# A recurrence with two dense layers: four more weight tiles converted behind the recurrence, and a new order on the vector engine and in the chunk loads

## The chip, the cores and the metric

One core of one Trainium2 chip runs the whole program. The metric is the device time of one execution in microseconds. Three executions of the kernel before took 1266.93, 1270.55 and 1269.22 us, with a median of 1269.22 us.

## The reference

Inputs are six tensors r, k, v, w, a, b of shape (4, 8, 768, 40) and the weights of two dense layers. Everything is float32 in the reference.

```python
# recurrence, for each batch and head; state is 40 x 40, t runs over 768 steps
y[t]  = r[t] @ state
Sa    = state @ a[t]
state = state * w[t][None, :] - outer(Sa, b[t]) + outer(v[t], k[t])
# x: y with heads side by side, 3072 tokens x 320
h = x @ w_in;  g = max(h, 0) ** 2;   x = g @ w_out     # first layer, 320 -> 2048 -> 320
h = x @ w_in2; g = h * cos(h);       out = g @ w_out2  # second layer, same sizes
```

The weights can arrive as float64, and then a 64-bit word is turned into a float32 on the chip by integer operations; this is the case here.

## The kernel before

**Recurrence.** The 768 steps are cut into 12 chunks of 64. Within a chunk the steps are put into matrix form, and a small triangular system per head has to be solved. `Program.period(c)` writes out chunk c as 42 slots; a list `todo` says which function is called in which slot. As no scheduler changes this order, an engine works through its instructions just as the calls emit them, and an instruction that waits holds up all that stand behind it on its engine or DMA queue. Nearly all DMAs are issued by SyncE (SP), so they form one list too.

In slots 0 to 16 and 20 to 36 the state update of chunk c runs in two halves (`Attn.state`, five stages each: tiles `pq`, `px`, `pu`, `py`, `pm` on TensorE, with ScalarE and VectorE between). In the same slots other chunks are prepared. For chunk c+1: the last Gram matrices (`gt`, tile `pgt`) are computed in slot 0 and masked by VectorE in slots 1 and 2, then written to DRAM (`gt_out`, tile `Ls`, slot 3) and read back in another layout (`solve_load`, tile `L`, slot 6). The triangular solve (`solve`, lines 472 and 475, 62 small operations and a copy) runs from slot 9 to slot 36, on VectorE for c = 0 and on GpSimd (POOL) after that. Its result goes to DRAM and back (`solve_store` and `load_t`, tiles `Tn`, `Ts`, `t`, `tt`, slots 37 and 38), and `merge` (tiles `pw`, `pt`) uses it in slot 2 of the next period. For chunk c+2: `load_kb` (line 362, 832 KB into `cin`, slot 7), `compact_kb` on VectorE (slots 10 to 16, line 404), `load_a` (slot 13). For chunk c+3: `load_w` (slot 30) and the first part of its decay products.

**Dense layers.** `Mlp.pipeline` handles 512 tokens at a time: six blocks for the first layer and then six for the second. Each block has 16 steps f, one for each 128 hidden units: 8 matmuls into `h` (input and weight are split into a high part and a rest, `xh`, `xl`), the activation (ScalarE and, for the rest `gl`, POOL), and two steps later the output matmuls `out(q - 2)`. The generator yields after pairs of matmuls; a period takes 64.2 of these yields, spread over its slots. The first layer's block b becomes ready after chunk 2b+1. `split_x` splits a block's input when the block before is at its last step: three ScalarE copies to `xh` and three VectorE subtractions to `xl`, in turn. Functions in `self.later` are called after a number of yields.

**Weights.** A tile is one f of one layer, 128 x 704 values. The first layer's tiles are converted in the first periods (`first`, `rest`). From the second layer's 16 tiles, `second` converts tiles 0 to 7 during the recurrence, in four pieces each: load (tile `w`), two ScalarE operations (lines 169 and 170), three VectorE operations (line 144 is the helper through which VectorE's instructions are recorded), one POOL addition (line 181), a store to DRAM (`w2f`, line 281). One piece starts every 5 steps of this generator, which is stepped in every slot for c = 2 and 3 and in every second slot after that. `load_w2` reads these tiles back in the first layer's last block. Tiles 8 to 15 are converted by `late` behind the recurrence, whole, one every 14 yields (tile `wr`), while the first layer's last block runs. `split_w2` splits each tile two steps ahead of its use in the second layer's first block: three VectorE and three POOL operations.

## Time and profile before

| What | us |
|---|---|
| median of three executions | 1269.22 |
| the profiled execution | 1271.16 |
| its span, first to last instruction | 1269.3 |
| start and periods 0 and 1, without dense layers | 0 to 211 |
| periods 2 to 10, with the first layer's blocks | 211 to 792 |
| period 11 | 792 to 843 |
| first layer's last block | 843 to 918 |
| second layer | 918 to 1262 |

TensorE is busy for 84% of the span, VectorE and ScalarE for 55% each and POOL for 52%. The granted TensorE clock is 0.905 on average: 0.61 to 0.95 in the periods, and full from period 11's end on. A period ends here where the store of the solve's result (`Tn`, line 485) is issued: at 69.9, 133.7, 211.4, 281.1, 348.1, 415.3, 479.0, 546.3, 607.7, 670.5, 732.4 and 792.3 us.

### The profile page before, as it was taken

What the parts mean: (1) busy time and instruction counts of PE and PEld (TensorE: products, weight loads), DVE (VectorE), ACT (ScalarE), POOL (GpSimd) and SP (SyncE); (2) the same over time, 40 slices, a digit from 0 to 9 for tenths busy, and PEclk for the clock granted to TensorE, in tenths of its full rate; (3) what the DMA queues carried; (4) which work ended last, traced back from release to release, by engine and by line L of the source; (5) the groups of instructions that cost most, each with busy time, mean ns of one, the idle gap of its engine ahead of it and who ended that gap; (6) DMA issues with size and microseconds to landing.
All of it is one profiled execution on the core that took longest, in us unless ns stands there. A gap on an engine that the chain in (4) does not pass through costs nothing.

```text
span 1269.3 us, 26741 instructions
## 1 busy us (share of the span) xinstructions
PE 1071.2 (84%) x10242; PEld 900.0 (71%) x10242; DVE 702.9 (55%) x1378; ACT 696.4 (55%) x1444; POOL 663.2 (52%) x1043
## 2 busy tenths in 40 slices
PE   3245626788979898988988989999999999999997
PEld 3144525666757676867776767777889999999996
DVE  6869856666655565655564543124696343443432
ACT  4133633656655556654846466447756565655553
POOL 4112486595938382848484838126796333333332
PEclk9985655788988888988989889899999999999999
DMA  6473653637282727463747262236201010100000
GB/s 177 89 166 100 152 140 65 139 87 149 60 187 83 150 66 156 104 132 87 159 105 148 54 137 71 58 99 216 70 12 46 1 47 1 47 13 34 1 22 25
DMA packets 271952, 115.96 MB, mean 91 GB/s; under 512 B 229990, under 2 KB 250982, under 8 KB 270670
## 3 DMA queue, kind: packets, MB, share of 16 engines
q1 hardware_dynamic: 269979, 113.47, 37.6%
q8 instruction: 83, 1.36, 0.4%
q10 hardware_dynamic: 1834, 0.69, 0.2%
q14 instruction: 56, 0.45, 0.1%
HBM read 88.42 MB, written 25.69 MB: 90 GB/s over the span
## 4 chain that ended last, share of the span: by engine, by line
PE 48%; POOL 20%; DMA 11%; DVE 10%; issue 5%; SPq 4%; ACT 2%; POOLq 0%; ACTq 0%; DVEq 0%
PE h L863 21%; PE pt L809 13%; POOL T L475 7%; PE po L819 6%; POOL ttmp L472 6%; DMA cin<-cin 6%; POOL gl L720 3%; POOL u L181 2%; DMA xf<-xs 1%; PE px L597 1%; DVE T L475 1%; DVE ttmp L472 1%; DMA t<-Tn 1%; DVE cin L144 1%; PE pu L605 1%
## 5 line engine op out<-in xcount | busy, mean ns | idle before, releaser
L863 PE MATMUL h<-xh,ws 128*128 128x512 f32 x960 | 332.1, 409 | 20.2 <-ACT g L717 18.0
L863 PE MATMUL h<-xl,ws 128*128 128x512 f32 x576 | 234.9, 408 | 0.5 <-DVE xl L144 0.5
L863 PEld LDWEIGHTS h<-xh,ws 128*128 128x128 f32 x960 | 184.9, 194 | 62.6 <-ACT g L717 20.1
L748 POOL TENSOR_TENSOR gl<-g,gh 128x512 fp32r<-128x512 f32 x96 | 125.1, 1303 | 191.0 <-ACT gh L747 158.9
L720 POOL TENSOR_TENSOR gl<-g,gh 128x512 fp32r<-128x512 f32 x96 | 126.8, 1320 | 186.5 <-ACT gh L719 146.0
L819 PE MATMUL po<-gh,ws 128*128 128x512 f32 x480 | 143.1, 422 | 1.9 <-ACT o L767 1.3
L472 POOL TENSOR_TENSOR ttmp<-T,L 128x126 f32<-128x126 f32 (+22 forms) x310 | 124.1, 400 | 35.7 <-DMA L<-Ls 15.3
L475 POOL TENSOR_TENSOR T<-T,ttmp 128x126 f32<-128x126 f32 (+22 forms) x310 | 128.7, 415 | 20.1
L717 ACT ACTIVATE g<-h 128x512 f32<-128x512 f32 x96 | 57.2, 596 | 134.2 <-PE h L863 92.5
L809 PE MATMUL pt<-ws,gh 128*128 128x320 f32 x768 | 128.1, 308 | 0.5 <-DVE g L144 0.4
L863 PEld LDWEIGHTS h<-xl,ws 128*128 128x128 f32 x576 | 111.9, 194 | 21.3 <-DVE xl L144 1.1
L181 POOL TENSOR_TENSOR u<-u,w 128x384 int32<-128x384 int32 (+2 forms) x72 | 54.7, 760 | 136.9 <-DVE u L144 108.9
L809 PEld LDWEIGHTS pt<-ws,gh 128*128 128x128 f32 x768 | 119.9, 188 | 8.3 <-DVE g L144 0.6
L144 DVE SCALAR_TENSOR_TENSOR g<-n,h 128x512 f32<-128x512 int32 x96 | 66.0, 688 | 103.2 <-ACT n L728 100.4
L728 ACT ACTIVATE n<-h 128x512 int32<-128x512 f32 x96 | 57.3, 596 | 119.9 <-PE h L863 119.8
L431 PE MATMUL pgt<-at,cin 40*128 40x104 f32 x768 | 70.7, 325 | 51.8 <-DVE at L144 21.0
L819 PEld LDWEIGHTS po<-gh,ws 128*128 128x128 f32 x480 | 94.0, 202 | 25.9 <-ACT o L767 1.9
L144 DVE TENSOR_SCALAR u<-u 128x160 f32<-128x160 f32 (+9 forms) x144 | 50.5, 351 | 99.7 <-ACT u L169 88.9
L144 DVE TENSOR_TENSOR g<-g,h 128x512 f32<-128x512 f32 x96 | 65.8, 685 | 71.7 <-ACT g L732 71.7
L144 DVE TENSOR_TENSOR mov<-pu,kc 64x416 f32<-64x416 f32 x96 | 56.5, 588 | 83.8 <-PE pu L606 81.4
L431 PEld LDWEIGHTS pgt<-at,cin 40*128 40x128 f32 x768 | 60.9, 226 | 58.6 <-issue 24.3
L819 PE MATMUL po<-gl,ws 128*128 128x512 f32 x288 | 85.9, 402 | 0.0
(104 smaller groups left out, 2310.2 us busy)
## 6 DMA issues: line engine op xcount, KB each, us to landing
w<-moe SPq DMA_DIRECT2D x20, 704.0 KB
rv<-rv SPq DMA_DIRECT2D x48, 256.0 KB
cin<-cin SPq DMA_DIRECT2D x11, 832.0 KB
Ls<-ga SPq DMA_DIRECT2D x48, 128.0 KB
L<-Ls SPq DMA_DIRECT2D x48, 128.0 KB
cin<-cin SPq DMA_DIRECT2D x11, 422.5 KB
at<-cin SPq DMA_DIRECT2D x11, 416.0 KB
mov<-vt SPq DMA_DIRECT2D x96, 40.0 KB
```

What stands on the lines that cost most here:

```text
L144: fn(*args, **kwargs)
L181: self.nc.gpsimd.tensor_tensor(t.bitcast(I32), u.bitcast(I32), w[:, :, 0], op=ALU.add)
L431: nc.tensor.matmul(pv[par][:, j], self.kb[r0:r0 + 40, p0 + j].rearrange("p h b -> p (h b)"), self.at[r0:r0 + 40, p0 + j], start=True, stop ...
L472: eng.tensor_tensor(tv, T[:, 0:r, j:j + 1].to_broadcast([128, r, n]), L[:, j:j + 1, j + 1:32].to_broadcast([128, r, n]), op=ALU.mult)
L475: eng.tensor_tensor(T[:, 0:r, j + 1:32], T[:, 0:r, j + 1:32], tv, op=ALU.add)
L717: nc.scalar.activation(g, h, AF.Relu)
L720: self.later.append((2, lambda: nc.gpsimd.tensor_tensor(gl, g, gh, op=ALU.subtract)))
L728: nc.scalar.activation(n, h, AF.Copy, bias=0.25, scale=float(np.float32(1.0 / (2.0 * np.pi))))
L748: nc.gpsimd.tensor_tensor(gl, g, gh, op=ALU.subtract)
L809: nc.tensor.matmul(self.pos[j][:, 0:DM], x[:, 128 * j:128 * j + 128], wo[:, DM * ws:DM * ws + DM], start=(f == 0 and x is gh and ws == 0), ...
L819: nc.tensor.matmul(self.pos[m], wo[:, 128 * ws:128 * ws + 128], x, start=(f == 0 and k in (0, 2, 4)), stop=(f == NF - 1 and k in (5, 6, 7)))
L863: nc.tensor.matmul(h, wi[:, ws], x[:, kt], start=(k == 0), stop=(k == 7))
```

## The change

`LATE` counts the tiles that `second` converts; it goes from 8 to 4, so `late` converts tiles 4 to 15. `load_w2` follows, as it reads back tiles below `LATE`. The vector operation that clamps a weight's high word moves from `clamp` to `bits`, for all weights, and the pieces' `bits` and `add` come one step later. `split_x` for the first layer (but for the very first block) puts its three subtractions off by four yields. The pipeline issues `out(q - 2)` ahead of the `h` matmuls at f = 0 of a first-layer block (not the first) instead of behind them; the list `later` no longer lets an entry that is not due hold up those behind it. `load_kb` moves from slot 7 to slot 1, `load_a` from 13 to 11, `load_w` from 30 to 18.

```diff
-LATE = 8
+LATE = 4
@@ class Weights: clamp, bits
         nc.scalar.activation(w[:, :, 0], w[:, :, 0].bitcast(U32), AF.Copy, scale=2.0 ** -29)
+
+    def bits(self, w, u):
+
+        hi, ui = w[:, :, 1], u.bitcast(I32)
         self.vec.tensor_scalar(u, u, LOW_WORD, HIGH_WORD, op0=ALU.max, op1=ALU.min)
-
-    def bits(self, w, u):
-
-        hi, ui = w[:, :, 1], u.bitcast(I32)
@@ pieces
-            return [(0, load), (4, clamp), (5, lambda: self.bits(st["w"], st["u"])),
-                    (6, lambda: self.add(st["w"], st["u"], st["u"])), (period + 5, lambda: end(f, c0, st["u"]))]
+            return [(0, load), (4, clamp), (6, lambda: self.bits(st["w"], st["u"])),
+                    (7, lambda: self.add(st["w"], st["u"], st["u"])), (period + 5, lambda: end(f, c0, st["u"]))]
@@ class Mlp: split_x(self, layer, blk, wait=0)
             nc.scalar.activation(xh[:, kt], xs[kt], AF.Copy)
-            self.vec.tensor_tensor(xl[:, kt], xs[kt], xh[:, kt], op=ALU.subtract)
+            if not wait:
+                self.vec.tensor_tensor(xl[:, kt], xs[kt], xh[:, kt], op=ALU.subtract)
+        if wait:
+            def low():
+                for kt in range(3):
+                    self.vec.tensor_tensor(xl[:, kt], xs[kt], xh[:, kt], op=ALU.subtract)
+
+            self.later.append((wait, low))
@@ stream
-                while self.later and self.later[0][0] <= 0:
-                    self.later.pop(0)[1]()
+                due = [fn for n, fn in self.later if n <= 0]
+                self.later = [z for z in self.later if z[0] > 0]
+                for fn in due:
+                    fn()
@@ pipeline
-            self.split_x(*steps[q][:2])
+            self.split_x(*steps[q][:2], 0 if steps[q][0] else 4)
...
             if q < len(steps):
+                if f == 0 and q and layer == 0:
+                    yield from out(q - 2)
...
-                if q >= 2:
+                if q >= 2 and (f or layer):
                     yield from out(q - 2)
@@ class Program: period
-            at(7, A.load_kb, c + 2)
-            at(13, A.load_a, c + 2)
+            at(1, A.load_kb, c + 2)
+            at(11, A.load_a, c + 2)
...
-            at(30, A.load_w, c + 3)
+            at(18, A.load_w, c + 3)
```

## Rows read from the trace of the kernel before

**Rows 1.** Page, part 4: shares of the chain that ended last, by engine.

```profile
PE 48%; POOL 20%; DMA 11%; DVE 10%; issue 5%; SPq 4%; ACT 2%; POOLq 0%; ACTq 0%; DVEq 0%
```

**Rows 2.** Window of period 8: length, busy us (count) per engine, clock, DMA share, GB/s.

```profile
607.70:670.50 62.80, 56.95 (x720) 45.52 (x717) 38.54 (x81) 40.42 (x92) 38.27 (x76) 0.95 0.59 132
```

**Rows 3.** Timeline of SP's DMA issues, 606 to 637 us: start, length, line, transfer.

```profile
607.73 0.49 SPq L485 DMA_DIRECT2D Tn<-L  x1
...
624.14 3.21 SPq L461 DMA_DIRECT2D L<-Ls  x4
...
628.63 0.45 SPq L362 DMA_DIRECT2D cin<-cin  x1
...
630.19 6.29 SPq L542 DMA_DIRECT2D mov<-vt  x2
```

**Rows 4.** Timeline of POOL in the same period: in brackets idle time before, releaser.

```profile
629.64 0.24 POOL L472 TENSOR_TENSOR ttmp<-T,L 128x31 f32<-128x31 f32 x1 [1.12 <-DMA L<-Ls]
...
641.30 0.74 POOL L181 TENSOR_TENSOR u<-u,w 128x256 int32<-128x256 int32 x1 [2.43 <-DVE u L144]
...
669.32 1.14 POOL L478 COPY L<-T 64x512 f32<-64x512 f32 x1
```

**Rows 5.** Timeline of VectorE: its wait for `cin` in period 8.

```profile
635.55 0.69 DVE L144 TENSOR_TENSOR cin<-cin 104x512 f32<-104x512 f32 x1 [6.16 <-DMA cin<-cin]
```

**Rows 6.** Windows around the load of `cin` in period 8.

```profile
614.60:629.60 15.00, 13.33 (x245) 10.62 (x246) 9.45 (x22) 13.37 (x29) 3.06 (x3) 1.00 0.92 208
629.60:634.60 5.00, 4.21 (x42) 3.25 (x37) 0.00 (x0) 2.71 (x6) 3.95 (x13) 1.00 0.82 188
634.70:641.50 6.80, 3.51 (x51) 3.06 (x52) 5.88 (x15) 2.74 (x8) 3.90 (x9) 0.66 0.74 172
```

**Rows 7.** Timeline of POOL: the same wait in periods 1 and 9.

```profile
164.61 1.02 POOL L181 TENSOR_TENSOR u<-u,w 128x384 int32<-128x384 int32 x1 [4.36 <-DVE u L144]
...
701.09 1.12 POOL L181 TENSOR_TENSOR u<-u,w 128x256 int32<-128x256 int32 x1 [3.50 <-DVE u L144]
```

**Rows 8.** TensorE's waits, whole span: total us, times, longest.

```profile
PE pm L638 <- DVE MT L144: 37.5, 15, 12.9
PE pw L511 <- DMA t<-Tn: 27.6, 18, 7.4
```

**Rows 9.** Line 181: ns min/median/max, first and last start.

```profile
L181 POOL TENSOR_TENSOR u<-u,w x72: 455/747/1843, 20.7 to 793.5; 128x160 int32<-128x160 int32 x24, 128x384 int32<-128x384 int32 x12, 128x320 int32<-128x320 int32 x12, 128x256 int32<-128x256 int32 x12
L181 POOL TENSOR_TENSOR wr<-wr,w x8: 1727/1733/2019, 857.2 to 902.4; 128x704 int32<-128x704 int32 x8
```

**Rows 10.** Timeline of SP: the load of a piece in period 8.

```profile
619.66 0.63 SPq L185 DMA_DIRECT2D w<-moe  x1
```

**Rows 11.** VectorE's waits between 70 and 735 us: total us, times, longest.

```profile
DVE u L144 <- ACT u L169: 87.7, 25, 10.9
DVE cin L144 <- DMA cin<-cin: 51.6, 10, 7.0
```

**Rows 12.** Windows around the second layer's start.

```profile
905.00:930.00 25.00, 24.65 (x122) 21.05 (x121) 19.80 (x31) 17.39 (x27) 21.42 (x25) 1.00 0.20 59
930.00:960.00 30.00, 30.00 (x167) 27.07 (x167) 29.43 (x42) 15.67 (x25) 28.14 (x34) 1.00 0.00 1
```

**Rows 13.** Timeline of VectorE: the last late tile (two of three operations), one split before and in the second layer.

```profile
897.38 3.02 DVE L144 TENSOR_SCALAR wr<-wr 128x704 f32<-128x704 f32 x2 [1.09 <-ACT wr L169]
...
914.27 0.28 DVE L144 TENSOR_SCALAR ws<-wr,kc 128x128 fp32r<-128x128 f32 x1
...
925.78 1.33 DVE L144 TENSOR_SCALAR ws<-wr,kc 128x128 fp32r<-128x128 f32 x1
```

**Rows 14.** Timelines of POOL and TensorE: a `gl` made, and its use.

```profile
925.66 1.36 POOL L748 TENSOR_TENSOR gl<-g,gh 128x512 fp32r<-128x512 f32 x1 [0.18 <-ACT gh L747]
...
928.77 0.75 PE L809 MATMUL pt<-ws,gl 128*128 128x320 f32 x4
```

**Rows 15.** Timeline of TensorE: start of the first layer's last block.

```profile
849.00 0.50 PE L863 MATMUL h<-xh,ws 128*128 128x512 f32 x1 [1.99 <-ACT xh L691]
```

More of the change, by code (lines that the diff above doesn't have):

```diff
@@ L170, in clamp @@
         nc.scalar.activation(w[:, :, 0], w[:, :, 0].bitcast(U32), AF.Copy, scale=2.0 ** -29)
-        self.vec.tensor_scalar(u, u, LOW_WORD, HIGH_WORD, op0=ALU.max, op1=ALU.min)
     def bits(self, w, u):
         hi, ui = w[:, :, 1], u.bitcast(I32)
+        self.vec.tensor_scalar(u, u, LOW_WORD, HIGH_WORD, op0=ALU.max, op1=ALU.min)
         self.vec.tensor_scalar(ui, ui, 0x07FFFFFF, 3, op0=ALU.bitwise_and, op1=ALU.logical_shift_left)
@@ L681, in load_x, with split_x @@
         self.xf[layer, self.key(blk)] = xs
-    def split_x(self, layer, blk):
+    def split_x(self, layer, blk, wait=0):
         nc = self.nc
```

## The prediction

> **What bounds the kernel now.** I read the chain of waits first [rows 1]: TensorE has under half of it, and POOL, DMA and SP together a third. A chain that was TensorE's alone from 862 us on and mixed before that calls for a reading by period. Period 8 is 62.8 us long; TensorE is busy in it for 56.95 us, but at a clock of 0.95 and partly with waits hidden in other engines' queues [rows 2]. So I followed one period around a closed loop. The solve's result is stored at 607.73; SP then issues DMA after DMA until it comes to the reads of `L` at 624.14 to 627.35 [rows 3]. POOL starts the next solve when `L` has landed, at 629.64, and works on it, with the `gl` and weight operations that stand between its steps, to 670.46 [rows 4]. That is 20.8 us from the copy's end at about 607.7 to landing plus 40.8 us of solve, which is the period but for its ends. In the first part the DMA engines are 92% busy [rows 6]; in the second POOL is, but for its short pauses and one long wait. TensorE does not set this loop: 27.6 us of its waits are for the result of the solve, which it needs as `t` at the head of a period [rows 8]. In the second layer TensorE is the bound: it is busy for 30.00 of 30 us at full clock [rows 12].
>
> So I price each edit by what it does to the loop of SP, DMA and POOL in periods 0 to 10, and to TensorE behind them.
>
> **The load of `cin` in slot 1.** Gain: before, SP issues it behind all reads of `L`, at 628.63 [rows 3]; VectorE, in order, waits 6.16 us for it at 635.55 [rows 5], ten such waits in the periods before 735 us being 51.6 us [rows 11]. Behind it stands a weight operation, and POOL's addition to the same tile waits for that in the middle of the solve: 2.43 us in period 8 [rows 4]. Such a wait is in the solves of periods 1 to 9, but for period 7: from 4.36 us in the first to 3.50 us in the last [rows 7], eight in all, whose mean I put at 2.8, so 22.6 us. Shorter waits of POOL for `gl` just behind them I put at 2 us. The load is then long there, so the 24.6 us go.
>
> Cost: the transfers of SP's list pass in the order of their issue; behind this load SP itself is stuck for most of 6.29 us in the issue of `mov` [rows 3]. In slot 1 the load stands ahead of `rv`, the block's `xf`, the `Ls` stores and the reads of `L`. Its 832 KB are 852 thousand bytes; at the 188 to 208 GB/s of the windows [rows 6] that is 4.1 to 4.5 us. The DMA engines have 8% free of the 15 us in which `L` has to come, 1.2 us, and somewhat more in periods without a block load. So `L` lands between 1.2 us (if twice the free time can be used, and the stores overlap) and 4.5 us later. I take 2.7 us, the transfer less the free time in periods of both kinds, for the nine periods from 1 to 9: 24.3 us, between 11 and 40. `rv`, `xf` and `mov` are late by the same, which TensorE can bear as long as it waits for `t` anyway. In period 0 VectorE runs the solve itself and waits for `cin` like in the others; it gains some 5 us and loses 2.7 to 4.5: I take -2, between -5 and +1. So the largest edit comes out near zero.
>
> The Trainium skill, page "DMA: Bandwidth & Descriptors", section "Rules for kernel authors", says to issue a DMA early and to wait for it late, since the setup is then covered. By that rule alone this edit would give all of the 24.6 us and the sum would be 1237. The rows speak against taking it so: in this stretch the engines that would cover the transfer are themselves 92% busy [rows 6].
>
> `load_a` and `load_w` move to places behind the reads of `L`, where nothing on the loop waits for them: 0, between -3 and +2. New waits on SP come with the moves (for TensorE's last `pgt` in slot 0, for ScalarE's copies in slot 10, for VectorE's last product in slot 16); what stands behind the first are the `Ls` stores, which need the result of the same `pgt`.
>
> **Sixteen pieces fewer in the recurrence.** At one piece per 5 steps the pieces now end in period 7, not at the start of period 11. Sixteen additions of POOL go, of 0.46 to 0.75 us [rows 9], some 9 us; by the time that solves have in periods 8 to 10 about ten of them stand in a solve: -6, between -9 and -3. On the way from the solve's end to `L` one piece per period stands in SP's list, such as that at 619.66 [rows 10]; load and store are 160 and 80 KB, 1.2 us of DMA at 208 GB/s. Three periods: -4, between -6 and 0. VectorE's 48 and ScalarE's 32 operations for them are off the loop: 0.
>
> **VectorE's order and the block change.** With the clamp behind the step in which ScalarE makes its input, 87.7 us of VectorE's waiting, 25 times, can go [rows 11]. VectorE is not on the loop but through the masks ahead of the `Ls` stores, and there SP's list is behind it: 0, between -8 and +2. `xl` four yields later: its consumer comes later too, since `out(q - 2)` now stands ahead of `h`. Those eight matmuls fill TensorE's wait at a block's start; in the last block, where TensorE is the bound, that wait is 1.99 us [rows 15]: -1.5. The price is that `h` of f = 1 now follows that of f = 0 at once and needs the same PSUM tile during the recurrence, so TensorE waits for ScalarE there; within the loop's slack: 0, between -2 and +4 for the four blocks.
>
> **Four tiles more behind the recurrence.** POOL's eight additions lie between 857.2 and 902.4, of 1.73 us [rows 9], one per 14 yields, so about 6 us apart. Four more fall between 908 and 927. There POOL is busy for 21.42 of 25 us and after that for 28.14 of 30 [rows 12], so of the 7 us, 3.6 find room and 3.4 pile up, to be taken off slowly. A `gl` made at 925.66 to 927.02 is used at 928.77 [rows 14], so the lag may be 1.75 us before TensorE waits: 1.6 us. VectorE, busy for 29.43 of 30 us [rows 12], gets three operations per tile, two of which took 3.02 us [rows 13] beside POOL's. I take +4 for both, between 0 and +10.
>
> The Trainium skill, page "SBUF — State Buffer", section "Who interferes with whom", says that VectorE in its two-port modes and POOL exclude each other for a whole instruction. The rows agree: the same 128x128 operation is 0.28 us at 914.27 and 1.33 us at 925.78, beside POOL's `gl` [rows 13]. By that rule VectorE's business here is mostly waiting for POOL, and every POOL addition put in lengthens VectorE's chain too; the sum would be that of the third rival.
>
> **Sum.** -24.6 + 24.3 - 2 - 6 - 4 - 1.5 + 4 = -9.8. The profiled execution took 1271.16 (its span 1269.3, and 1.9 around it), which makes 1261.4. It lies 1.9 above the median of 1269.22, which would make 1259.4; I say 1260.
>
> **Rivals.**
>
> First: the wait for `cin` costs more than POOL's part shows. Stage `pm` waits for VectorE behind it, 37.5 us in 15 waits [rows 8], some 23 of them in periods 3 to 9, and the clock falls to its lower level behind such a gap: 0.66 over the 6.8 us from 634.7 [rows 6], so about 4.6 us at 1.2 GHz. If TensorE set the period, 23 us and six times 3 us would go: about 1269 - 41 + 4 - 4 = 1228. Against it: TensorE waits for `t` in most periods, so time that it gains it would give back there.
>
> Second, on the other side: `L` is late by the whole transfer, 4.5 us in nine periods, as SP's list has a read that must wait for the `Ls` store, and the free time of the DMA engines lies ahead of it. Then the first edit costs 40.5 - 24.6, and the sum is +6.4: 1276. It is slower than before from a delay of 3.8 us on, where 9 x 1.1 eats the 9.8. For it: the SP list is dense, and DMA at 92%. Against it: odd periods have no `xf` and more free time.
>
> Third: the second layer's start takes 10 us, not 4, and the first edit is 3 us worse: 1269, no change. It decides where POOL's lag passes the 1.75 us at the first of the four tiles.
>
> **How the numbers follow.** The forecast gets 0.47, the first rival 0.12, the second 0.21, the third 0.20. A difference of 0.3%, 3.8 us, is about what a measurement of this kernel can tell from none. Faster: 0.42 of the forecast's and 0.12, 0.54. Within it: 0.22, most of the third rival and an edge of the forecast. Slower: 0.24, the second rival and some of the third. The forecast's own range is 1248 to 1268 (the first edit's delay, 2.7 by one up or down, is 9 us). The range that holds 8 in 10 goes up to the second rival, 1277, and down half of the way to the first, 1238.
>
> **What would show it.** Right: VectorE's waits for `cin` near zero; POOL without a long wait for `u` within a solve; the landing of `L` some 3 us later behind the solve's store, so that a period up to 7 keeps its length within 2 us; periods 8 to 10 shorter by 3 to 5 us; `h` of the last block without its 1.99 us; VectorE and POOL saturated between 905 and 965, and TensorE with a few us of waits there. Wrong: periods 2 to 7 shorter by 4 us or more each (then TensorE's path set them), or longer by 2 or more (then `L` is late by all of the transfer).

## The result, and the profile after

The kernel after takes 1284.97 us (median of 4, 1281.59 to 1289.15) beside 1269.37 us before (median of 4): a ratio of 1.0124, with a 95% interval from 1.0103 to 1.0146. It is slower by 15.6 us; the prediction was 1260 us, faster. The profiled execution took 1289.15 us, its span is 1287.4, which is 18.1 more than before. Up to the last load of `xf` in the recurrence (843.3 us before, 849.5 after) 6.2 of these are lost in the two profiles, behind it 11.9.

The chain that ended last has less of POOL than before and more of TensorE, DMA and VectorE [rows 1]:

```profile
PE 51%; POOL 16%; DMA 12%; DVE 11%; SPq 4%; issue 3%; ACT 3%; POOLq 0%; ACTq 0%; DVEq 0%
```

SP's timeline in period 8 (start, length, line, transfer) shows the moved load in the place where [rows 3] had none. The reads of `L` now start 19.9 us behind the solve's store, not 16.4:

```profile
618.19 0.49 SPq L485 DMA_DIRECT2D Tn<-L  x1
...
625.10 1.23 SPq L362 DMA_DIRECT2D cin<-cin  x1
...
626.77 2.83 SPq L677 DMA_DIRECT2D xf<-xs  x4
...
638.08 2.74 SPq L461 DMA_DIRECT2D L<-Ls  x4
640.92 1.16 SPq L463 DMA_DIRECT2D l<-Ls  x2
```

POOL in the same period, to be read beside [rows 4]: the wait for `u` inside the solve is gone, the solve takes 41.3 us (643.33 to 684.62) in place of 40.8, since a wait for `gl` has come into it; and it starts 25.1 us behind the store, not 21.9.

```profile
643.33 0.24 POOL L472 TENSOR_TENSOR ttmp<-T,L 128x31 f32<-128x31 f32 x1 [3.38 <-DMA L<-Ls]
...
647.59 1.27 POOL L727 TENSOR_TENSOR gl<-g,gh 128x512 fp32r<-128x512 f32 x1 [2.70 <-ACT gh L726]
...
683.27 1.35 POOL L478 COPY L<-T 64x512 f32<-64x512 f32 x1
```

The first stretch of this period in two windows (columns as in [rows 2]): the DMA engines are as full as in [rows 6], still so when `L` is being read, and TensorE's granted clock falls to 0.50 there, its lower level of 1.2 GHz:

```profile
619.00:638.00 19.00, 11.19 (x176) 9.10 (x176) 5.66 (x11) 6.88 (x14) 0.39 (x1) 0.72 0.91 190
638.00:644.00 6.00, 5.08 (x52) 4.56 (x53) 2.88 (x7) 3.91 (x9) 1.78 (x4) 0.50 0.92 171
```

TensorE's waits (total, times, longest): `pm` no longer waits for VectorE, but `pw` waits more for the solve's result, and `pu` for the copies `tt`, which is new [rows 8].

```profile
PE pw L511 <- DMA t<-Tn: 40.0, 16, 8.1
PE pu L605 <- ACT tt L528: 22.3, 6, 6.6
...
PE pm L638 <- DVE MT L144: 6.5, 4, 4.5
```

At the second layer's start, the same two windows as in [rows 12]: TensorE, which was busy all the time, now is for 22.39 of 25 and 24.27 of 30 us, at a clock of 0.89 in the second.

```profile
905.00:930.00 25.00, 22.39 (x95) 17.28 (x94) 22.11 (x24) 17.18 (x27) 20.55 (x18) 1.00 0.35 118
930.00:960.00 30.00, 24.27 (x119) 21.37 (x119) 27.07 (x39) 14.85 (x24) 24.12 (x27) 0.89 0.14 46
```

What it waits for stands in VectorE's list. A late tile's operations (`wr`) come between the two halves of an activation, and TensorE has to wait for the second (timelines of VectorE, then of TensorE):

```profile
932.15 1.87 DVE L144 TENSOR_SCALAR wr<-wr 128x704 f32<-128x704 f32 x2
934.06 0.89 DVE L144 SCALAR_TENSOR_TENSOR wr<-w,wr 128x704 int32<-128x704 int32 x1
934.86 0.68 DVE L144 TENSOR_TENSOR g<-g,h 128x512 f32<-128x512 f32 x1
```

```profile
921.69 0.50 PE L874 MATMUL h<-xl,ws 128*128 128x512 f32 x1 [1.15 <-DVE xl L144]
...
935.60 0.90 PE L818 MATMUL pt<-ws,gh 128*128 128x320 f32 x2 [4.68 <-DVE g L144]
```

### The profile page after: what moved, and what is told of

Read it like the earlier page. It is cut to its first block, busy times and chain, and to the rows that moved or that the text cites. A ratio compares the mean times of both kernels' runs of the same rounds, so it can differ in the third digit from the quotient of the medians.

```text
span 1287.4 us, 26555 instructions
## 1 busy us (share of the span) xinstructions
PE 1074.6 (83%) x10242; PEld 899.5 (70%) x10242; DVE 704.7 (55%) x1342; ACT 694.1 (54%) x1420; POOL 663.7 (52%) x1031
## 4 chain that ended last, share of the span: by engine, by line
PE 51%; POOL 16%; DMA 12%; DVE 11%; SPq 4%; issue 3%; ACT 3%; POOLq 0%; ACTq 0%; DVEq 0%
PE h L874 21%; PE pt L818 12%; PE po L828 7%; POOL T L475 5%; POOL ttmp L472 5%; DMA xf<-xs 3%; POOL gl L727 2%; DMA Ls<-ga 2%; DVE lam L144 2%; DMA cin<-cin 2%; DMA t<-Tn 2%; PE pgt L431 2%; DVE T L475 1%; DVE cin L144 1%; DVE ttmp L472 1%
## 5 line engine op out<-in xcount | busy, mean ns | idle before, releaser
L472 POOL TENSOR_TENSOR ttmp<-T,L 128x126 f32<-128x126 f32 (+22 forms) x310 | 123.4, 398 | 57.9 <-DMA at<-cin 16.8
L475 POOL TENSOR_TENSOR T<-T,ttmp 128x126 f32<-128x126 f32 (+22 forms) x310 | 129.8, 419 | 19.7
L818 PE MATMUL pt<-ws,gh 128*128 128x320 f32 x768 | 128.9, 310 | 5.1 <-DVE g L144 4.7
L818 PEld LDWEIGHTS pt<-ws,gh 128*128 128x128 f32 x768 | 120.5, 189 | 13.4 <-DVE g L144 4.9
L181 POOL TENSOR_TENSOR u<-u,w 128x160 int32<-128x160 int32 (+4 forms) x56 | 46.8, 835 | 96.9 <-DVE u L144 87.3
L739 ACT ACTIVATE g<-g,kc 128x512 f32<-128x512 f32 x96 | 69.7, 726 | 26.7 <-DVE g L144 26.6
```

Source lines behind the costliest of these rows:

```text
L472: eng.tensor_tensor(tv, T[:, 0:r, j:j + 1].to_broadcast([128, r, n]), L[:, j:j + 1, j + 1:32].to_broadcast([128, r, n]), op=ALU.mult)
L475: eng.tensor_tensor(T[:, 0:r, j + 1:32], T[:, 0:r, j + 1:32], tv, op=ALU.add)
L739: nc.scalar.activation(g, g, AF.Sin, bias=self.kc[:, K_QT:K_QT + 1])
L818: nc.tensor.matmul(self.pos[j][:, 0:DM], x[:, 128 * j:128 * j + 128], wo[:, DM * ws:DM * ws + DM], start=(f == 0 and x is gh and ws == 0), ...
```

## The experiments

All ratios are to the kernel before, run in the same rounds on the same chip. The other columns are from the profile of each: POOL's ten solves (first to last instruction, as in [rows 4], added up), the nine pauses between them, the waits for `u` inside the solves, the issue of the last read of `L` behind the solve's end (mean of nine), and the tail from the last load of `xf` to the end; all in us.

| kernel | ratio, 95% interval | solves | pauses | `u` | last `L` | tail |
|---|---|---|---|---|---|---|
| before | 1 | 433.6 | 201.6 | 22.6 | 20.1 | 425.9 |
| after | 1.0124 (1.0103 to 1.0146) | 418.3 | 221.8 | 0 | 23.2 | 437.8 |
| three loads alone | 1.0058 (1.0034 to 1.0083) | 417.6 | 226.4 | 0.3 | 22.9 | 426.5 |
| twelve late tiles alone | 1.0020 (0.9995 to 1.0046) | 429.3 | 200.0 | 15.5 | 20.0 | 439.7 |
| VectorE's order alone | 1.0050 (1.0027 to 1.0072) | 439.4 | 208.4 | 19.1 | 20.4 | 426.0 |
| block change alone | 1.0033 (1.0011 to 1.0054) | 446.7 | 196.6 | 19.2 | 19.8 | 428.0 |
| after, `cin` in slot 7 | 1.0092 (1.0056 to 1.0128) | 441.1 | 198.3 | 21.3 | 20.2 | 438.0 |
| after, `cin` in slot 3 | 1.0131 (1.0103 to 1.0159) | 406.4 | 233.4 | 0 | 24.0 | 437.9 |
| before, `cin` in quarters | 0.9871 (0.9836 to 0.9906) | 420.0 | 198.6 | 0 | 19.7 | 428.6 |
| after, `cin` in quarters | 0.9872 (0.9843 to 0.9901) | 416.4 | 195.0 | 1.1 | 19.9 | 438.7 |
| before, quarters and `xf` early | 0.9790 (0.9765 to 0.9815) | 420.1 | 194.1 | 0 | 19.0 | 425.4 |

One caution first: four of the kernels below (twelve late tiles alone, and the three others with twelve under "The tail") have the same instructions up to the last load of `xf`, and reach it at 831.8, 834.8, 840.7 and 842.1 us; their solves and pauses add up to between 629.3 and 637.3 us. So a difference of 8 to 10 us in the recurrence between single profiles proves nothing. The tail is steadier: 425.2 to 428.6 us in the ten kernels with eight late tiles, 437.8 to 441.1 in the seven with twelve whole ones. The ratios come from four to twelve executions of each kernel.

**The parts one by one.** First the early load was taken out of the change, the late tiles were taken out of it, and each of the two was put alone into the kernel before.

```diff
-            at(1, A.load_kb, c + 2)      # in the kernel after
+            at(7, A.load_kb, c + 2)
```

> The kernel after, but the load of cin is back in slot 7, behind the reads of L. Theory A (the load ahead of the block's xf makes xf land late, ScalarE waits for it in order, and the merge's copies tt behind it keep TensorE waiting at the head of the even periods): the even periods 2, 4, 6 and 8, which are 3.3, 5.8, 3.7 and 3.7 us longer in the kernel after, lose these 16.5 us, the waits of pu for tt fall from 22.3 us to about 3; the waits for cin come back and cost up to the 24 us that the prediction gave them, most of it in odd periods. Net 1270 to 1285. Rival (the reads of L, late by the transfer, are what costs): all periods from 1 to 9 gain 1 to 3 us each, odd ones as well, and the time is 1265 to 1270. Rival (the load costs nothing, all of the loss is in the tail): 1285 to 1310, since the waits for cin come back and nothing is won.

Measured 1.0092. The even periods 4, 6 and 8 lose 6.2, 5.4 and 2.7 us, as theory A had it, and the waits for `u` are back (21.3 us). But period 2 loses nothing, and the waits of `pu` for `tt` stay at 16.9 us, where theory A had about 3. By the two ratios the early load accounts for the smaller part of the loss: 0.0092 of 0.0124 stays without it, though the intervals overlap.

```diff
-LATE = 4                                 # in the kernel after
+LATE = 8
```

> The kernel after, but with eight weight tiles behind the recurrence, as before. Theory B (the four tiles more collide with VectorE's and POOL's work at the second layer's first block): the tail from the last load of xf to the end falls from 437.9 us to about 426, and the periods 8 to 10, which are 3.8, 1.3 and 2.9 us shorter in the kernel after, give back some 8 us with the pieces that return. Net 1278 to 1284. Rival (the tail is longer for the order of VectorE's work and for xl put off, not for the tiles): the tail stays at 436 to 438 and the time goes to 1290 to 1296.

Measured 1.0110 (1.0074 to 1.0146). The tail falls to 427.1, as theory B said; the recurrence takes 13.4 us more up to the last load of `xf`, so little is left. (The 3.8, 1.3 and 2.9 us that the expectation quotes are those of periods 9, 10 and 11; period 8 is 3.7 us longer in the kernel after.)

```diff
-            at(7, A.load_kb, c + 2)      # in the kernel before
-            at(13, A.load_a, c + 2)
+            at(1, A.load_kb, c + 2)
+            at(11, A.load_a, c + 2)
@@
-            at(30, A.load_w, c + 3)
+            at(18, A.load_w, c + 3)
```

> The kernel before, with the three chunk loads in the slots of the change and nothing else. Theory A: the even periods 2 to 8 are longer by 3 to 6 us each, odd ones within 2 us, xh waits for xf for 25 us or more in all (12.4 before) and pu for tt 20 us or more (2.8 before); the waits for cin fall under 10 us; the tail stays at 426. Time 1275 to 1288. Rival (the reads of L late by the whole transfer): every period from 1 to 9 is longer by 1 to 2 us, 1278 to 1285, with odd periods like even ones. Rival (the loads are neutral, as the prediction had it): 1266 to 1272.

Measured 1.0058, 7.4 us. The solves get 16.0 us shorter and the pauses 24.8 us longer. Periods 4, 6 and 8 are 5.8, 3.0 and 3.8 us longer, the odd ones from 3 on change by less than 2, as theory A said, and `xh` waits 25.1 us for `xf`. But `pu` waits 2.6 us for `tt` (2.8 before), not 20 or more: a late `xf` alone does not bring that wait. On POOL, between 150 and 800 us, the waits for `u` shrink, from this in the kernel before,

```profile
POOL u L181 <- DVE u L144: 35.5, 14, 10.1
```

and those for `l`, the second part of `L`, are new:

```profile
POOL ttmp L472 <- DMA L<-Ls: 14.2, 3, 10.7
POOL u L181 <- DVE u L144: 13.9, 6, 10.1
...
POOL ttmp L472 <- DMA l<-Ls: 10.8, 4, 5.2
```

```diff
-LATE = 8                                 # in the kernel before
+LATE = 4
```

> The kernel before, with twelve tiles behind the recurrence rather than eight and nothing else. Theory B: the tail from the last load of xf is 8 to 12 us longer than 426, with waits of pt for g and of h for xl between 910 and 950; the periods 8 to 10 are 5 to 10 us shorter for the pieces that go. Net 1267 to 1274. Rival (the prediction's terms, 4 us lost in the tail and 10 won in the recurrence): 1260 to 1265. Rival (the tail is long only with the changed order of VectorE): the tail stays under 430 and the time is 1260 to 1264.

Measured 1.0020, 1274.38 us, at the upper end of what theory B says: in the profiles the recurrence gains 11.5 us and the tail loses 13.8. The parts so far, 7.4 and 2.5 us, explain 10 of 15.6. So the two that the prediction had at nothing were run alone.

```diff
-        self.vec.tensor_scalar(u, u, LOW_WORD, HIGH_WORD, op0=ALU.max, op1=ALU.min)   # clamp
...
+        self.vec.tensor_scalar(u, u, LOW_WORD, HIGH_WORD, op0=ALU.max, op1=ALU.min)   # bits
@@
-            return [(0, load), (4, clamp), (5, lambda: self.bits(st["w"], st["u"])),
-                    (6, lambda: self.add(st["w"], st["u"], st["u"])), (period + 5, ...
+            return [(0, load), (4, clamp), (6, lambda: self.bits(st["w"], st["u"])),
+                    (7, lambda: self.add(st["w"], st["u"], st["u"])), (period + 5, ...
```

> The kernel before, with VectorE's clamp moved behind ScalarE's two operations (one step later, with the operations that follow it) and nothing else. In the kernels measured so far, some 8 us of the recurrence are not accounted for by the loads and the tiles: the kernel after with eight late tiles reaches the last load of xf at 862.9, the kernel before with the loads alone at 855.0. Theory C1 (the order of the weight operations costs it: they now stand one step later in VectorE's list, and with them POOL's additions in the solve): the recurrence is 6 to 10 us longer than the 843.3 of before, in all periods, also in 0 and 1 where the first layer's block does not run; time 1275 to 1282. Theory C2 (the block change costs it): this run stays within 3 us, 1267 to 1273. The prediction had 0, between -8 and +2.

Measured 1.0050, 6.4 us, as theory C1 had it, with a tail of 426.0. The change of places does halve VectorE's waits for ScalarE's `u`, as predicted (88.9 to 45.9 us up to the last load of `xf`), and it costs time all the same. Between 290 and 560 us ScalarE and TensorE wait longer than in the kernel before. ScalarE, before and then here (64.0 and 81.1 us over the whole span):

```profile
ACT ws L208 <- POOL u L181: 7.0, 2, 5.5
```

```profile
ACT ws L208 <- POOL u L181: 16.8, 5, 5.6
```

TensorE, before and then here:

```profile
PE h L863 <- ACT g L717: 4.9, 1, 4.9
```

```profile
PE h L863 <- ACT g L717: 11.9, 5, 5.2
```

```diff
-                if q >= 2:
+                if q >= 2 and (f or layer):   # and out(q - 2) ahead of h at f == 0
@@
-        self.split_x(*steps[q][:2])
+        self.split_x(*steps[q][:2], 0 if steps[q][0] else 4)
```

> The kernel before, with the block change alone (xl four yields later, the output stage of the step before last ahead of h). Theory C1 (order): within 3 us of before, 1267 to 1273, the recurrence at 843 and the tail at 424 to 426. Theory C2 (TensorE waits at f = 1 for ScalarE to free the PSUM tile of h, and in the recurrence nothing stands between them any more): the odd or even periods in which a block begins are 1 to 3 us longer, 8 us in all, the recurrence ends at 851, and the time is 1273 to 1280. The prediction had 0 in the recurrence, between -2 and +4, and -1.5 in the last block.

Measured 1.0033, 4.2 us. The 1.99 us of [rows 15] are gone, but the output stage, now at the head, has to wait longer itself. TensorE's timeline at that place, before and then here:

```profile
860.73 1.22 PE L819 MATMUL po<-gh,ws 128*128 128x512 f32 x4 [1.29 <-ACT o L767]
862.55 0.50 PE L819 MATMUL po<-gh,ws 128*128 128x512 f32 x1 [0.60 <-DVE o L144]
```

```profile
865.18 2.08 PE L828 MATMUL po<-gh,ws 128*128 128x512 f32 x4 [3.13 <-ACT o L774]
```

By these waits the last block gains some 0.8 us, not 1.5. But behind the 3.13 us TensorE's granted clock is 0.50 from 865.18 to 868.87 us, where the kernel before has 1.00 all through this block, and the tail is 428.0 us, not 425.9: no gain is left. In the recurrence the solves are 13.1 us longer and the pauses 5.0 shorter. The time is what theory C2 says, but its cause is not seen: between 150 and 800 us TensorE's waits of `h` for ScalarE's `g` are 15.4 us, and were 18.0.

**Which half of these two.** Two halves were run: the clamp moved with the later operations left in their steps, and the output stage moved without putting off `xl`.

```diff
+        self.vec.tensor_scalar(u, u, LOW_WORD, HIGH_WORD, op0=ALU.max, op1=ALU.min)   # in bits, still step 5
```

> The kernel before, with VectorE's clamp put behind ScalarE's operations into the step of the other two operations, but these and POOL's addition left in their steps (5 and 6, in the change 6 and 7). Theory (the cost of the new order is that POOL's addition stands one step later, closer to what waits for it: ScalarE's split of the tile and SP's load into the same buffer): ScalarE's waits for u fall back from 81.1 to about 64 us, SP's loads of w behind u from 75.9 to about 59, and the time is 1268 to 1274. Rival (the clamp's own place costs it, since VectorE now has three dependent operations in one go ahead of the masks): as with the whole order, 1276 to 1282.

Measured 1.0035 (1.0007 to 1.0063): neither the whole cost nor none. Of the two waits named, ScalarE's came back to 64.0 us and SP's stayed at 76.3.

```diff
+                if f == 0 and q and layer == 0:
+                    yield from out(q - 2)
```

> The kernel before, with the output stage put ahead of h at a block's start, but xl made at once. Theory (the block change costs 4 us because h of the second tile now follows h of the first at once and waits for ScalarE to free their one PSUM tile, and with it the waits of POOL for gl grow): as much as the whole block change, 1274 to 1280, recurrence 845 to 850. Rival (xl put off by four yields is what costs): 1267 to 1273.

Measured 1.0021 (0.9996 to 1.0045), inside the interval of the whole block change and of no change; its solves, 445.7 us, are as long as with the whole. Which half costs is not settled.

**What stands behind the load.** In slot 3 the load is behind `xf` and still ahead of `L`.

```diff
-            at(1, A.load_kb, c + 2)
+            at(3, A.load_kb, c + 2)
```

> The kernel after, but the load of cin in slot 3: behind the block's xf in SP's list, still ahead of the reads of L. Theory A (xf late is what lengthens the even periods): periods 4, 6 and 8 fall by 3 to 6 us each, and xh waits for xf for some 15 us, not 27.4; odd periods stay; the waits for cin stay under 15 us; time 1270 to 1276, better than the 1284 of slot 7, which has these waits. Rival (L late by the transfer is what costs): as the reads of L stand behind the load here too, no period gets shorter, 1282 to 1288.

Measured 1.0131. Theory A falls as an account of the net loss. `xf` is no longer late (the waits of `pu` for `tt`, between 150 and 800 us, are 3.9 us, not 22.3), and nothing is gained, for the reads of `L` take the delay. SP's timeline in period 9 shows it. In the kernel before, the four reads need 4.53 us to be issued there, and in the periods 0 to 9 between 2.88 and 6.68 us:

```profile
683.86 4.53 SPq L461 DMA_DIRECT2D L<-Ls  x4
```

Here they need 7.23 us, and between 6.5 and 10.0 in the ten periods:

```profile
692.33 0.71 SPq L362 DMA_DIRECT2D cin<-cin  x1
...
695.96 7.23 SPq L461 DMA_DIRECT2D L<-Ls  x4
703.29 1.96 SPq L463 DMA_DIRECT2D l<-Ls  x2
```

POOL's waits for `L` between 150 and 800 us, with no wait for `u` left in the solves:

```profile
POOL ttmp L472 <- DMA L<-Ls: 45.9, 6, 12.8
POOL ttmp L472 <- DMA l<-Ls: 22.2, 4, 8.0
```

It is one list, and the load costs its transfer to whatever stands behind it.

**The load where the DMA engines are idle.** In the last part of the solve of period 7 they are 28% busy in the kernel before (window, columns as in [rows 2]):

```profile
585.00:607.70 22.70, 22.17 (x258) 17.84 (x258) 11.76 (x27) 12.26 (x29) 19.99 (x43) 1.00 0.28 80
```

The tile is in use there, but by quarters: the products `pgt` read it in four parts, three of them in that stretch. So three quarters can be loaded in the period before, each behind its last reader.

```diff
+    def load_kbq(self, c, m):
+        a, b = W65 + 512 * m, W65 + 512 * m + 512
+        self.nc.sync.dma_start(self.cin[:, a:b], self.i["cin"][c, :, a:b])
@@
-            at(7, A.load_kb, c + 2)
+            if c == 0:
+                at(7, A.load_kb, c + 2)
+            else:
+                at(7, A.load_kbq, c + 2, 3)
@@
+            for m, t in enumerate((26, 34, 36)):
+                at(t, A.load_kbq, c + 3, m)
```

> The kernel before, with the load of cin cut into four parts: three are issued in the period before, each behind the product that last reads its part, so that they pass during the solve, and only the fourth stays behind the reads of L. It keeps the gain of the early load and takes its cost away. Theory L (the early load gives back POOL's waits for u, 22.6 us in the solves, and costs as much because the reads of L land 3 us later in each period, 23.2 us between solves and 5.1 us in them, as the loads alone showed): here the waits for u fall to about 4 us, the reads of L are issued as early as before (15.6 us behind the solve's end, 18.8 in the loads alone), solve and pause together fall from 635.4 to about 615, and the time is 1250 to 1258. Rival (a period is set by another path, so that the time won in the solve is lost elsewhere, late L or not): solve and pause stay over 628 and the time is 1266 to 1275.

Measured 0.9871, 1255.88 us, within the range expected. The waits for `u` in the solves are gone and `L` is not late (SP's timeline of period 8; line numbers are four higher in this kernel):

```profile
593.50 0.48 SPq L489 DMA_DIRECT2D Tn<-L  x1
...
610.50 3.06 SPq L465 DMA_DIRECT2D L<-Ls  x4
613.65 1.35 SPq L467 DMA_DIRECT2D l<-Ls  x2
615.06 0.45 SPq L366 DMA_DIRECT2D cin<-cin  x1
...
630.91 0.35 SPq L366 DMA_DIRECT2D cin<-cin  x1
```

Solves and pauses together fall by 16.6 us, and the median by 16.8. That is two thirds of the gain that the prediction gave the early load (24.6 us), without its cost. That the two numbers agree so well is partly luck, given the scatter of single profiles. The same edit on the kernel after:

> The kernel after, with the load of cin in four parts, three of them in the period before. If the parts of the change add up (order 6.4, block 4.2, late tiles 2.5 us alone, 13.1 together, and the load in parts gives 16.8), it takes 3 to 4 us less than before, 1266 to 1272. Rival (their costs are hidden once L is in time, or cost through the wait for cin alone): 1256 to 1262, as the load in parts by itself. Rival (they cost more where the loop is shorter): over 1274.

Measured 0.9872, 1257.56 us, the first rival: what is left of the change neither costs nor gives anything there. Its tail is 10 us longer and its recurrence 6 us shorter than with the quarters alone. So the 6.4 and 4.2 us of the two reorderings are no fixed price. They were measured in a kernel in which VectorE waits for `cin` in the solve; whether that wait makes them, the runs don't show.

The block's `xf` was then put ahead of the solve's store too, into the same idle stretch:

```diff
+        if c % 2 and more:
+            at(37, self.M.load_x, 0, c // 2)
@@
-            if c % 2 == 0 and c and t == 2:
-                self.M.load_x(0, c // 2 - 1)
```

> The kernel before with the load of cin in parts, and the block's xf loaded in slot 37 of the period before, behind the store of y and ahead of the solve's store, not in slot 2. Theory L (whatever stands in SP's list between the solve's store and the reads of L delays the next solve): in periods 4, 6, 8 and 10 the reads of L are issued 3 us earlier, and these periods are 2 to 4 us shorter, 8 to 14 us in all; the time is 1242 to 1250. Rival (xf, issued just ahead of the solve's store, now delays that store by its own transfer): nothing won, 1253 to 1262.

Measured 0.9790, 1247.69 us: another 0.8%. The profiles show only part of it: solves and pauses fall by 4.4 us and the tail by 3.2, and one pause, in period 4, is 5.1 us longer. SP's timeline in period 8 has `xf` 4.35 us ahead of the store, and the reads of `L` start 13.4 us behind it, in place of 17.0 with the quarters alone.

```profile
590.65 2.58 SPq L681 DMA_DIRECT2D xf<-xs  x4
595.00 0.49 SPq L489 DMA_DIRECT2D Tn<-L  x1
...
608.44 4.09 SPq L465 DMA_DIRECT2D L<-Ls  x4
612.63 1.13 SPq L467 DMA_DIRECT2D l<-Ls  x2
```

**The tail.** Four runs varied the late tiles in the kernel before.

```diff
-        return self.stages([job(f) for f in range(LATE, NF)], 14)   # with LATE = 4
+        return self.stages([job(f) for f in range(LATE, NF)], 10)
```

> The kernel before with twelve tiles behind the recurrence, one per 10 yields in place of 14, so that the last ends before the second layer's first block. Theory B (the late tiles collide with VectorE's and POOL's work at that block): the tail falls from the 439.7 of twelve tiles at one per 14 to between 426 and 431, the recurrence keeps its gain of 11.5, and the time is 1259 to 1266, faster than before. Rival (the tiles cost the same wherever they stand, since POOL and VectorE are then the bound of the whole tail): the tail stays above 436, 1270 to 1276.

Measured 1.0031 (1.0014 to 1.0048); the tail is 441.1 us. The last addition now starts at 917.6 us, not 931.3, so theory B fails: the tiles cost as much there. TensorE's longest wait between 860 and 950 us is now for `xl` of the second layer's first block:

```profile
PE h L863 <- DVE xl L144: 6.0, 1, 6.0
```

```diff
-LATE = 8
+LATE = 6
```

> The kernel before, with ten tiles behind the recurrence in place of eight or twelve. Theory B (a threshold: the tiles cost nothing until they reach the second layer's first block, at about 905 us, where VectorE and POOL have no room): the last two of ten end near 906, the tail is 427 to 432, the recurrence gains half of the 11.5 us of twelve tiles, and the time is 1264 to 1270. Rival (each tile costs the same, 3.4 us of tail): the tail is 433, the time 1270 to 1275, as for eight and twelve.

Measured 0.9996 (0.9973 to 1.0018): a tail of 429.4, as theory B had it, and no gain that could be measured. With the run before it, theory B's threshold is neither shown nor ruled out: ten tiles cost less than their share, twelve earlier ones no less.

```diff
-            return [(0, load), (8, clamp), (12, lambda: self.bits(st["w"], st["u"])),
-                    (17, lambda: self.add(st["w"], st["u"], st["u"]))]
+            out = [(0, load), (8, clamp), (12, lambda: self.bits(st["w"], st["u"])),
+                   (17, lambda: self.add(st["w"], st["u"], st["u"]))]
+            return out if f < NF - 4 else out[:2] + out[3:]     # and clamp without VectorE
+            return out if f < NF - 4 else out[:3]               # the other run
```

> The kernel before with twelve tiles behind the recurrence, of which the last four (tiles 12 to 15) leave out VectorE's three operations; the rest of them is as in the run with twelve tiles, whose tail is 439.7 us. Theory V (VectorE, in order, waits for ScalarE at each late tile, and xl and g of the second layer's first block stand behind it): the tail falls to 428 to 432, and the time to 1262 to 1266. Rival (POOL's additions delay gl and the split of the tiles): the tail stays over 436, 1270 to 1275. Both would show as half each, about 434.

> The kernel before with twelve tiles behind the recurrence, of which the last four leave out POOL's addition, VectorE's and ScalarE's operations staying. Theory V (VectorE's order): the tail stays over 435. Rival (POOL's additions): the tail falls to 428 to 432 and the time to 1262 to 1266.

Measured 0.9973 (0.9954 to 0.9993) with a tail of 432.3, and 0.9993 (0.9971 to 1.0016) with 435.1, beside 1.0020 and 439.7 with all operations. By the tails VectorE's part is the larger (7.4 us), and POOL's is not nothing (4.6); the times do not reach the 1262 to 1266 us of either theory. In the windows from 910 to 925 us TensorE's busy time and granted clock follow the same order. In turn: before, twelve tiles, without VectorE's operations, without POOL's.

```profile
910.00:925.00 15.00, 14.65 (x71) 12.33 (x71) 10.86 (x19) 10.31 (x17) 11.92 (x15) 1.00 0.33 98
```

```profile
910.00:925.00 15.00, 9.37 (x37) 7.66 (x36) 9.92 (x14) 6.87 (x12) 10.89 (x11) 0.77 0.30 95
```

```profile
910.00:925.00 15.00, 12.26 (x53) 9.96 (x52) 9.43 (x16) 10.90 (x17) 12.54 (x13) 0.93 0.45 133
```

```profile
910.00:925.00 15.00, 10.24 (x43) 8.38 (x42) 10.26 (x15) 6.81 (x11) 8.36 (x11) 0.89 0.36 123
```

**Is anything of the change worth keeping?** The kernel after with both loads moved into the idle stretch, with twelve and with eight late tiles:

> The kernel after, with the load of cin in quarters and xf in the period before. Theory L and what the change on top of the quarters showed (1257.6 beside 1255.9 without it): the remaining parts cancel, the recurrence is some 6 us shorter for the pieces that go and the tail 12 us longer, so 1245 to 1254, not better than the kernel before with the same two loads (1247.7). Rival (pieces fewer in SP's list are worth more in a shorter loop): 1236 to 1243.

> As the run beside it, with eight late tiles as in the kernel before, so that of the change only the order of VectorE, the block change and the places of two small loads are left. Theory (these cost 6.4 and 4.2 us alone): 1250 to 1258, a tail of 426 and a recurrence of 823 to 830. Rival (they cost nothing when L is in time): 1244 to 1249, as the kernel before with the two loads. Rival (only now do they gain): under 1243.

Measured 0.9847 (0.9817 to 0.9877) and 0.9826 (0.9796 to 0.9856), 1252.56 and 1250.80 us; tails of 440.2 and 428.6. Neither is better than 0.9790 for the kernel before with the same two loads, which is the fastest version found. The second tests the two reorderings without the tiles: it takes 0.0036 more than that kernel, about 4.6 us, with some 5 us of doubt either way by the two intervals, and 3.2 us of it stand in the tail. So the two cost less here than the 10.6 us that they cost alone; that they cost nothing is not shown.

## Why the prediction was wrong, point by point

Four terms failed, all in the same direction: the gain of the early load (24.6 us, where the solves gave back 16.0), the price of the late tiles (+4, measured 13.8 and 10.7), and the two reorderings, put at 0 and -1.5 and measured at +6.4 and +4.2.

**The loop of SP, DMA and POOL** was the right object. Where the reads of `L` were kept in time, solves and pauses fell by 16.6 us and the time by 16.8. (Its first part in period 8, from 607.73 to 629.64, is 21.9 us, not the 20.8 of the prediction.) The first rival, that TensorE sets the period, falls: `pm`'s waits for VectorE went (37.5 to 6.5 us) and the periods got no shorter, as `pw` waited for `t` instead (27.6 to 40.0). Of the prediction's own signs, those for "right" came at VectorE (waits for `cin` 59.4 to 8.5 us) and POOL (no wait for `u`); one for "wrong" came too, as periods 2, 4 and 6 are 3.3, 5.8 and 3.7 us longer.

**The load of `cin`, gain.** Right in mechanism, too large in size. The waits for `u` in the solves were 22.6 us and went. But the solves fell by 16.0, not by 24.6, in the loads alone: POOL's own operations took longer there (line 472, 124.1 to 128.9 us for 310 of them; why, no run shows), and the waits for `gl` went down by one microsecond, not two.

**The load of `cin`, cost.** Right in mechanism and nearly in size: `L` was to be late by 2.7 us in nine periods; its last read was issued 2.8 us later in the loads alone and 3.1 in the kernel after, and the pauses grew by 24.8 and 20.2 us, where the prediction had 24.3. (The last of the nine pauses is at the head of period 10, which has no such load; in the other eight the read is 3.3 and 3.7 us later.) The Trainium skill's rule to issue a DMA early, so that its setup is covered (page "DMA: Bandwidth & Descriptors", section "Rules for kernel authors"), gives the edit its whole gain as the prediction read it: the runs disagree in this list (+7.4 us), and give 16.8 of the 24.6 us where the load passes in the idle stretch. That TensorE can bear a late `xf` held: in the loads alone `xh` waits 25.1 us for it and `pu` only 2.6 for `tt`. The 22.3 us of `pu` in the kernel after stay at 16.9 with the load back in slot 7 and are 10.3 with the block change alone. The three loads were not run apart, so that the places of `load_a` and `load_w` cost nothing is not shown. The term as a whole was put at -2.3 us with period 0, and measured +7.4 (4.3 to 10.6 by its interval).

**Sixteen pieces fewer**: -10 us, right. In single profiles the gain of the recurrence scatters from 1.2 to 11.5 us over four kernels that are alike up to there; the difference in time less that of the tail gives 10 to 11 us in all four.

**The late tiles, +4 us (0 to +10)**: this term failed most plainly, as it was mis-sized threefold: 13.8 us alone, 10.7 in the change, far outside the scatter of the tails. The four additions more were to fall between 908 and 927 us; the last started at 931.3 alone and at 947.5 in the kernel after. The sum counted what VectorE's and POOL's operations add where an engine is nearly full. It left out that these operations stand ahead of `xl` and `g` in an ordered list, that one activation late stops TensorE for 4.68 us at once, and that the clock drops after such gaps: 0.77 and 0.89 in the windows above. The prediction had the row in hand (VectorE busy for 29.43 of 30 us [rows 12]) and read from it how much room there was, not what stood behind. How much each of these three takes is not shown.

**VectorE's order, 0, and the block change, -1.5**: alone +6.4 and +4.2. The 87.7 us of waiting [rows 11] that were to go did halve, and were worth nothing, as the prediction said; the last block's 1.99 us [rows 15] came back as a longer wait of the output stage (3.13 us in the block change alone, 2.66 in the kernel after) with the clock at 0.50 and 0.53 for 3.6 us behind it, which the prediction didn't price. That both would be free in the recurrence was wrong in the kernel before; +2 and +4 were its bounds. The first moves waits in ordered lists onto others (`ws` and `h`), but that these make the 6.4 us is argued, not shown: with the later steps left in place ScalarE's wait was back at 64.0 us and the ratio still 1.0035. What makes the block change's cost in the recurrence stays open.

By the runs alone the four parts are off by 9.7, 8.5, 6.4 and 5.7 us, all in one direction: 30 together, where the whole was off by 25, so the parts don't simply add up. The second rival, at 1276, named a late `L` as its cause; the time went past it because the tail and the two orders came on top.

## What to carry to other kernels

A transfer that moves ahead in a full list is paid for by whatever stands behind it there; look in the windows for the stretch in which the DMA engines have room (here 28% busy, in the solve) and ask which part of the buffer is free by then: here three quarters of it were. Work added to an engine that is 98% busy is to be priced by what stands behind it in the list and by the clock that the gap costs, not by the room that the average leaves. A reordering "off the critical path" deserves a run of its own: two of them cost 0.3 to 0.5% each here, and together less than that sum once the loads passed elsewhere.

## What was not expected of the hardware

Reads can be held up in their issue: the four DMAs of `L` took SP 6.5 to 10.0 us close behind the load of `cin` and 2.88 to 6.68 without it in front, so a large transfer delays not only what lands but also what SP does next. VectorE's two passes over a late tile's 128x704 values took, in the kernel after, 3.03 us at 903.67, with POOL busy beside them, and 1.09 at 942.04, with POOL idle. And one wait of TensorE of 4.68 us, in the kernel after, was followed by a clock of 0.50 from 935.6 to 940 us, with TensorE busy all that time, 0.77 from 940 to 943 and 1.00 after that. At half the clock for some 5.8 us (an estimate from these windows) the gap cost about 2.9 us more than its length.
